# Score blocks of 64 queries by 192 keys, one bias product per PSUM bank, and the attention output copied out of PSUM by VectorE

## The chip, the cores and the metric

The kernel runs on one core of a Trainium2 chip. The metric is the device time of one execution in microseconds; the times shown are medians of a few runs. A core has five engines that run side by side and meet only at semaphores: TensorE (PE in the profile; its weight loads are PEld), VectorE (DVE), ScalarE (ACT), GpSimd (POOL) and SyncE (SP), which issues most of the transfers. Every engine works through its own instructions in the order in which they were written.

## The reference

For 8 batches and 8 heads there are 576 queries of width 64. A query sees itself and the 127 keys before it, with a penalty that grows with the distance and a slope for each head. The result goes through a soft mixture of experts with 8 experts of 4 slots.

```python
scores = scale * np.matmul(q, k.transpose(0, 1, 3, 2))
rel = pos[:, None] - pos[None, :]
bias = slopes[:, None, None] * (-np.abs(rel))[None, :, :]
mask = (rel >= 0) & (rel < window)                 # window = 128
scores = np.where(mask, scores + bias[None], -1000000000.0)
attn = softmax(scores)                             # rows
x = (attn @ v)                                     # all heads side by side: (4608, 512)

logits = x @ phi                                   # 32 slots
d = softmax(logits, axis=0); slot_input = d.T @ x
slot_out[e] = np.maximum(slot_input[e] @ w1[e], 0) @ w2[e]
return softmax(logits, axis=1) @ slot_out
```

## The kernel before, in words

A batch is cut into five tiles of queries: t = 0 to 3 with 128 queries, t = 4 with 64. A *group* is a tile and four of its heads (t < 4, g = 0 or 1), or tile 4 with all eight heads. There are nine groups a batch and 72 in all, and the main loop does one per iteration `i`, from about 9 to 210 us. The expert products and the output follow; they are not touched.

The scores of a group fill two PSUM banks, `s4s[i % 2]`, 128 partitions by 4 x 256 columns. Heads come in pairs: of a pair, one head lies on partitions 0 to 63 of the transposed queries and keys, the other on 64 to 127 (`par` in the code, which is also the bank), and `jj` counts the pairs of a group. For t > 0 the queries are cut into four strips of 32, and each strip meets 160 keys (`WIN = P + KB`), its own 32 and the 128 before. A strip has its own 32 of TensorE's columns, so its tile of the array is 64 rows by 32 columns, and eight tiles work side by side. Eight bias products with bf16 operands (`ones`, `ramp`; L259) start the sums, one for each strip and bank with 2 x 160 columns; then 16 f32 products of 160 columns follow (L266), each of which the trace shows as two. For t = 0 the 128 queries are one piece (L247, L252).

Since the strips are shifted against each other, each row's 128 valid keys lie in a ring of 256 columns. `merge` (L281 for t = 1 to 3, L283 for t = 4) folds the two halves into 128 columns by a predicated copy in PSUM. For t = 0 there are no older keys, and `merge` (L279) writes a very low number, `low`, over the keys that come after the query.

The rest of an iteration is a software pipeline in `softmax_front`, `expo`, `flip`, `split` and `values`:

- VectorE: `merge`, row maximum (`rowmax`, L301), reciprocal of the previous group's row sums (L313), the exponential's bias (L304), and the normalisation of the previous group's probabilities (L317).
- ScalarE: `split` of the group three back (L379, the flipped probabilities out of PSUM), the copies of the expert part (`x_keep`, L447, and others), `x_store` (L426), then four exponentials with row sums (L357).
- GpSimd: the row sums' total (L309), and two selects (L381, L383; for t = 4 L386, L388) that part the split probabilities into those of the tile's own keys and those of the tile before.
- TensorE: `flip` of the group three back (L372), `values` of the group four back (L410), the scores of the next group, then the expert part's products: `x_flip` (L438), `logits` (L456), `slot_sum` (L514).

`values` adds the two or four head pairs of a group into one PSUM bank `xp` for each tile. There is one such bank. When a tile's last group is done, `x_store` copies it to SBUF (37 times in the loop), and the next tile's `values` write the bank again. `x_store` is called by `after_values` behind `values`; without an engine in its call it uses VectorE. The loop body sets the order on every engine:

```python
if i:
    softmax_front(new, groups[i - 1])
...
flip(groups[i + near - FLAG]); split(groups[i + near - FLAG])
run("act", i)
values(groups[i + near - LAG]); after_values(i, groups[i + near - LAG])
scores(i + 1)
loads(i + 1)
expo(new)
run("pe", i); load_weights_at(i); run("dve", i)
```

`near` is 1 for the first seven iterations and 0 after; FLAG is 3 and LAG is 4. `run` issues what the expert part of a *pass* (four tiles together) has due in this iteration.

Of the kernel before, what the change touches and what calls it, by code (L numbers as in the profile page):

```python
# [10 lines left out]
F32 = mybir.dt.float32  # L11
# [13 lines left out]
P = 128  # L25
# [5 lines left out]
LOW = -1e30  # L31
# [3 lines left out]
KB = 32  # L35
# [33 lines left out]
def tile_attn_softmoe(  # L69
# [20 lines left out]
    mask_u = cst[:, 0:P].bitcast(I32)  # L90
    mask_t = cst[:, P:P + TAIL].bitcast(I32)
# [14 lines left out]
    ramp = cpool.tile([P, 2, 2, WIN], BF16, name="ramp")  # L106
    ones = cpool.tile([P, P], BF16, name="ones")
    area = cpool.tile([P, 19, HW], F32, name="area")

    kall = kq[:, 0:NB * P].rearrange("p (n j w) -> p n j w", n=NB, j=NPAIR)  # L110
    qs = [kq[:, NB * P + 2 * P * i:NB * P + 2 * P * i + 2 * P] for i in range(3)]
# [94 lines left out]
    with tc.manual_schedule(engines=ORDERED):  # L206
        warm = area[:, 2].bitcast(BF16)[:, 0:512]
        nc.vector.memset(warm, 0.0)
        nc.vector.memset(low, LOW)
        nc.vector.memset(ramp, 0.0)  # L210
        nc.vector.memset(ones, 1.0)
        nc.vector.memset(fine[:, 10:11], -1.0)
        nc.gpsimd.memset(cst[:, 0:P], 1.0)
        nc.gpsimd.affine_select(cst[:, 0:P], cst[:, 0:P], [[1, P]], ALU.is_gt, 0.0, base=0, channel_multiplier=-1)
        load_k(0, 0)
        load_q(0, nc.scalar)
        for par in range(2):
            nc.sync.dma_start(ramp[64 * par:64 * par + 1], slopes[par:par + 1])
# [12 lines left out]
        load_v()  # L231
        nc.scalar.dma_start(cst[:, P:], cstd)
        nc.scalar.dma_start(phi, phid)
        for t in range(2, NT):
            load_k(0, t)

    def scores(i):
        b, t, g = groups[i]
        s4 = s4s[i % 2]
        parts = [s4[:, 0:2], s4[:, 2:4]]  # L240
        if i == 0:
            parts = [ps_1.tile([P, 2, 2 * P], F32, tag="xp", name="s4_0"), pq[:, 0].rearrange("p (u w) -> p u w", u=2)]
            parts = parts[::-1]
        qt = qs[i % 3].rearrange("p (j w) -> p j w", w=width(t))
        if t == 0:
            for par, rows in enumerate(half):
                nc.tensor.matmul(  # L247
                    parts[par][:, :, 0:P], lhsT=ones[rows], rhs=ramp[rows, g, :, 0:P],
                    start=True, stop=False)
            for jj in range(2):  # L250
                for par, rows in enumerate(half):
                    nc.tensor.matmul(  # L252
                        parts[par][:, jj, 0:P], lhsT=qt[rows, jj], rhs=kall[rows, 0:4, 2 * g + jj],
                        start=False, stop=(jj == 1))
        else:
            strips = [(c // 2, c % 2) if t == 4 else (g, c) for c in range(4)]
            for par, rows in enumerate(half):
                for c, (h, r) in enumerate(strips):
                    nc.tensor.matmul(  # L259
                        s4[32 * c:32 * c + 32, 2 * par:2 * par + 2, 32 * r:32 * r + WIN],  # L260
                        lhsT=ones[rows, 0:32], rhs=ramp[rows, h], start=True, stop=False)
            for jj in range(2):
                for par, rows in enumerate(half):
                    for c, (h, r) in enumerate(strips):
                        m0 = 4 * (t - 1) + r
                        nc.tensor.matmul(  # L266
                            s4[32 * c:32 * c + 32, 2 * par + jj, 32 * r:32 * r + WIN],
                            lhsT=qt[rows, 2 * h + jj if t == 4 else jj, 32 * r:32 * r + 32],
                            rhs=kall[rows, m0:m0 + 5, 2 * h + jj], start=False, stop=(jj == 1))
        st[groups[i]] = {"s4": s4, "parts": parts}  # L270

    ALL, LO, HI = slice(0, 4), slice(0, 2), slice(2, 4)

    def merge(key, us=ALL):
        t = key[1]
        s4 = st[key]["s4"]
        if t == 0:
            m = len(range(4)[us])
            nc.vector.copy_predicated(merged(key, us), bc(mask_u, 1, m), bc(low, 1, m).to_broadcast([P, m, P]))  # L279
        elif t < 4:  # L280
            nc.vector.copy_predicated(s4[:, :, P:2 * P], bc(mask_u, 1, 4), s4[:, :, 0:P])  # L281
        else:
            nc.vector.copy_predicated(s4[:, :, 0:TAIL], bc(mask_t, 1, 4), s4[:, :, P:P + TAIL])  # L283
# [12 lines left out]
    def rowmax(key, us):
        if "mx" not in st[key]:
            o = P - merged_at(key)
            st[key]["mx"] = st[key]["s4"][:, :, o] if number[key] else work.tile([P, 4], F32, tag="mx", name="mx")
            st[key]["nb"] = work.tile([P, 4], F32, tag="nb", name="nb")  # L300
        nc.vector.tensor_reduce(st[key]["mx"][:, us], merged(key, us), axis=AX.X, op=ALU.max, negate=True)  # L301
# [49 lines left out]
    def expo(key, us=ALL):  # L351
        s = st[key]
        if "sm" not in s:
            s["p4"] = p4s[number[key] % 3]
            s["sm"] = work.tile([P, 4], F32, tag="sm", name="sm")
        for u in range(4)[us]:
            nc.scalar.activation(  # L357
                s["p4"][:, u], merged(key, u), AF.Exp,
                bias=s["nb"][:, u:u + 1], scale=SCALE, accum_out=s["sm"][:, u:u + 1],
            )  # L360

    def flip(key, us=ALL, to=None):
        s = st[key]
        if to is not None:
            s["pt"] = to.rearrange("p u (r w) -> p u r w", r=2)
            for u in range(4)[us]:
                nc.tensor.transpose(to[:, u], s["p4"][:, u], ident)
            return
        s["pt"] = pq_p.rearrange("p r (u w) -> p u r w", u=4)
        for u in range(4)[us]:  # L370
            for r, rows in enumerate(half):
                nc.tensor.transpose(s["pt"][:, u, r], s["p4"][rows, u], ident[rows, rows])  # L372

    def split(key, us=ALL):
        s, t = st[key], key[1]
        i = number[key] % 2 if number[key] < n - 1 else 2
        m = len(range(4)[us])
        pa, pp = pas[i], pps[i % 2]
        nc.scalar.copy(pa[:, us].rearrange("p u (r w) -> p u r w", r=2), s["pt"][:, us])  # L379
        if 0 < t < 4:  # L380
            nc.gpsimd.affine_select(  # L381
                pp[:, us], pa[:, us], [[0, m], [-1, P]], ALU.is_gt, 0.0, base=0, channel_multiplier=1)
            nc.gpsimd.affine_select(  # L383
                pa[:, us], pa[:, us], [[0, m], [1, P]], ALU.is_ge, 0.0, base=0, channel_multiplier=-1)
        elif t == 4:
            nc.gpsimd.affine_select(  # L386
                pp[:, us], pa[:, us], [[0, m], [0, 2], [-1, TAIL]], ALU.is_gt, 0.0, base=0, channel_multiplier=1)
            nc.gpsimd.affine_select(  # L388
                pa[:, us], pa[:, us], [[0, m], [0, 2], [1, TAIL]], ALU.is_ge, 0.0, base=0, channel_multiplier=-1)
        s.update(pd=pa, pp=pp)  # L390

    def values(key, pairs=None, to=None):
# [5 lines left out]
        pd, pp = st[key]["pd"], st[key]["pp"]  # L398
# [5 lines left out]
        for ph in parts:  # L404
            for i in inner:
                j = 2 * g + i
                for par in range(2):
# [4 lines left out]
                        rhs=src[:, 2 * par + i] if t < 4 else src[:, 2 * par + i % 2, TAIL * (i // 2):TAIL * (i // 2) + TAIL],  # L412
# [323 lines left out]
    def after_values(i, key):  # L736
# [8 lines left out]
        x_store(b, t, nc.scalar)  # L745
# [28 lines left out]
    with tc.manual_schedule(engines=ORDERED):  # L774
# [60 lines left out]
        split(gd, LO)  # L835
# [6 lines left out]
        split(gd, HI)  # L842
# [280 lines left out]
```

## Time and profile before

| | |
|---|---|
| median of 3 runs | 289.46 us (289.28 to 292.43) |
| the profiled execution | 288.49 us, its span 286.0 us |
| TensorE, VectorE, ScalarE, GpSimd busy | 253.9, 221.6, 205.6, 112.9 us |
| granted TensorE clock, mean | 0.982 |
| HBM | 251 GB/s over the span |

A row of the groups names line, engine, operation, output and input tile, with shapes as partitions x elements and the count. Behind the bar stand the busy time in us, the mean of one in ns, and the engine's idle time just ahead, with what ended it. For a product, 64*32 means 64 rows by 32 columns of weights. A row of the timeline has start, duration, engine and line, with the idle time in brackets; several instructions of one line are merged, with their count. A product's end is modelled, and the next one can begin before it. In a row of waits stand the total in us, the count and the longest. In the windows' row stand the length and the busy time of PE, PEld, DVE, ACT and POOL, then clock, DMA share and GB/s. "issue" is idle time for which the profile shows no reason.

### The profile page before, as it was taken

What the parts mean: (1) busy time and instruction counts of PE and PEld (TensorE: products, weight loads), DVE (VectorE), ACT (ScalarE), POOL (GpSimd) and SP (SyncE); (2) the same over time, 40 slices, a digit from 0 to 9 for tenths busy, and PEclk for the clock granted to TensorE, in tenths of its full rate; (3) what the DMA queues carried; (4) which work ended last, traced back from release to release, by engine and by line L of the source; (5) the groups of instructions that cost most, each with busy time, mean ns of one, the idle gap of its engine ahead of it and who ended that gap; (6) DMA issues with size and microseconds to landing.
All of it is one profiled execution on the core that took longest, in us unless ns stands there. A gap on an engine that the chain in (4) does not pass through costs nothing.

```text
span 286.0 us, 13588 instructions
## 1 busy us (share of the span) xinstructions
PE 253.9 (89%) x5535; PEld 178.9 (63%) x5535; DVE 221.6 (77%) x509; ACT 205.6 (72%) x817; POOL 112.9 (39%) x218
## 2 busy tenths in 40 slices
PE   8588999799979889989979998998979899999990
PEld 4366676676757567667657765766756443687750
DVE  2889989998997999988998998798973352656451
ACT  2888889988888988998898988888783411044460
POOL 2044626662573276257527725466552011000000
PEclk9689999999999999999999999999999999999997
DMA  6645368869885987969797978866574579998997
GB/s 184 218 134 164 100 197 270 276 195 289 285 271 152 305 297 233 278 224 305 218 286 242 328 236 251 278 204 219 165 265 140 169 254 365 411 393 322 362 384 282
DMA packets 36754, 72.61 MB, mean 254 GB/s; under 512 B 4402, under 2 KB 15316, under 8 KB 36692
## 3 DMA queue, kind: packets, MB, share of 16 engines
q1 hardware_dynamic: 35972, 71.24, 75.7%
q8 instruction: 43, 0.70, 1.0%
q10 hardware_dynamic: 720, 0.51, 0.6%
q14 instruction: 19, 0.16, 0.2%
HBM read 62.29 MB, written 9.44 MB: 251 GB/s over the span
## 4 chain that ended last, share of the span: by engine, by line
PE 45%; DVE 23%; ACT 16%; POOL 7%; issue 5%; DMA 2%; DVEq 0%; ACTq 0%; POOLq 0%
ACT area L357 9%; PE xp L410 7%; DVE area L317 6%; DVE s L301 6%; PE s L266 5%; PE op L967 5%; PE hp L930 5%; PE po L992 4%; DVE s L281 3%; POOL area L381 3%; PE pq L372 3%; PE lp L456 2%; DVE s L279 2%; PE s L259 2%; ACT area L379 2%
## 5 line engine op out<-in xcount | busy, mean ns | idle before, releaser
L357 ACT ACTIVATE area<-s,nb 128x128 f32<-128x128 f32 x286 | 102.7, 391 | 13.8 <-DVE nb L304 10.4
L410 PE MATMUL xp<-area 128*64 128x128 f32 (+1 forms) x1104 | 74.5, 272 | 8.4 <-POOL area L381 5.3
L357 ACT ACTIVATION_READ_ACCUMULATOR area<-s,nb 128x1 f32 x286 | 65.4, 229 | 0.0
L410 PEld LDWEIGHTS xp<-area 128*64 128x64 f32 x1104 | 54.1, 137 | 18.0 <-POOL area L381 6.1
L317 DVE TENSOR_TENSOR area<-area,rs 128x512 f32<-128x512 f32 (+1 forms) x73 | 61.0, 836 | 1.6
L301 DVE TENSOR_REDUCE s<-s 128x4 f32<-128x512 f32 x71 | 49.5, 697 | 2.2
L379 ACT COPY area<-pq 128x512 f32<-128x512 f32 (+1 forms) x72 | 43.5, 605 | 10.7 <-PE pq L372 9.0
L266 PE MATMUL s<-kq 64*32 64x160 f32 x1792 | 43.8, 302 | 2.3 <-issue 2.3
L309 POOL TENSOR_SCALAR rs<-sm 128x4 f32<-128x4 f32 x70 | 15.0, 214 | 73.0 <-ACT area L357 71.6
L383 POOL TENSOR_SCALAR_AFFINE_SELECT area<-area 128x512 f32<-128x512 f32 x48 | 41.7, 870 | 3.3
L381 POOL TENSOR_SCALAR_AFFINE_SELECT area<-area 128x512 f32<-128x512 f32 x48 | 35.5, 740 | 15.5 <-ACT area L379 14.6
L281 DVE COPY_PREDICATED s<-cst,s 128x512 f32<-128x512 int32 x48 | 33.1, 689 | 6.1 <-PE s L266 5.6
L372 PE MATMUL pq<-unit_r,area 64*128 64x64 f32 x552 | 31.3, 233 | 3.7 <-ACT area L322 2.8
L266 PEld LDWEIGHTS s<-kq 64*32 64x32 f32 x1792 | 30.1, 107 | 4.1 <-issue 3.5
L372 PEld LDWEIGHTS pq<-unit_r,area 64*128 64x128 f32 x552 | 23.3, 140 | 11.8 <-issue 3.2
L259 PE MATMUL s<-ramp,ones 64*32 64x320 bf16 x448 | 18.7, 311 | 4.8 <-ACT area L357 4.5
L426 ACT COPY area<-xp 128x512 f32<-128x512 f32 (+1 forms) x37 | 21.4, 578 | 0.2
L447 ACT COPY area<-pq 128x512 f32<-128x512 f32 x34 | 20.7, 608 | 0.3 <-PE pq L432 0.3
L438 PEld LDWEIGHTS pq<-unit_r,area 64*128 64x128 f32 x264 | 11.1, 137 | 12.8 <-issue 9.7
L994 ACT COPY ob<-po 128x512 f32<-128x512 f32 x19 | 10.4, 591 | 11.4 <-PE po L992 11.4
L994 DVE COPY ob<-po 128x512 f32<-128x512 f32 x17 | 11.2, 686 | 6.6 <-PE po L992 6.5
L438 PE MATMUL pq<-unit_r,area 64*128 64x64 f32 x264 | 15.2, 233 | 0.9 <-ACT area L379 0.6
(173 smaller groups left out, 329.1 us busy)
## 6 DMA issues: line engine op xcount, KB each, us to landing
w<-w SPq DMA_DIRECT2D x53, 512.0 KB, 5.5
out<-ob SPq DMA_DIRECT2D x36, 256.0 KB, 3.9
kq<-q_t SPq DMA_DIRECT2D x69, 128.0 KB, 3.5
kq<-k_t SPq DMA_DIRECT2D x32, 256.0 KB, 3.9
area<-v_n SPq DMA_DIRECT2D x31, 256.0 KB, 4.2
area<-w SPq DMA_DIRECT2D x8, 512.0 KB, 4.6
area<-v_n SPq DMA_DIRECT2D x12, 128.0 KB, 4.4
kq<-w SPq DMA_DIRECT2D x3, 512.0 KB, 5.9
```

What stands on the lines that cost most here:

```text
L259: nc.tensor.matmul(s4[32 * c:32 * c + 32, 2 * par:2 * par + 2, 32 * r:32 * r + WIN], lhsT=ones[rows, 0:32], rhs=ramp[rows, h], start=True, ...
L266: nc.tensor.matmul(s4[32 * c:32 * c + 32, 2 * par + jj, 32 * r:32 * r + WIN], lhsT=qt[rows, 2 * h + jj if t == 4 else jj, 32 * r:32 * r + 32],
L281: nc.vector.copy_predicated(s4[:, :, P:2 * P], bc(mask_u, 1, 4), s4[:, :, 0:P])
L301: nc.vector.tensor_reduce(st[key]["mx"][:, us], merged(key, us), axis=AX.X, op=ALU.max, negate=True)
L317: nc.vector.tensor_tensor(p4, p4, bc(rs, 2, P), op=ALU.mult)
L357: nc.scalar.activation(s["p4"][:, u], merged(key, u), AF.Exp, bias=s["nb"][:, u:u + 1], scale=SCALE, accum_out=s["sm"][:, u:u + 1],)
L372: nc.tensor.transpose(s["pt"][:, u, r], s["p4"][rows, u], ident[rows, rows])
L379: nc.scalar.copy(pa[:, us].rearrange("p u (r w) -> p u r w", r=2), s["pt"][:, us])
L381: nc.gpsimd.affine_select(pp[:, us], pa[:, us], [[0, m], [-1, P]], ALU.is_gt, 0.0, base=0, channel_multiplier=1)
L383: nc.gpsimd.affine_select(pa[:, us], pa[:, us], [[0, m], [1, P]], ALU.is_ge, 0.0, base=0, channel_multiplier=-1)
L410: nc.tensor.matmul(xp[D * par:D * par + D, j, 0:w], lhsT=v_slot[b, t - 1 + ph][:, D * h:D * h + D], rhs=src[:, 2 * par + i] if t < 4 else ...
L438: nc.tensor.transpose(xq[:, j, r], x[rows, j], ident[rows, rows])
```

## The change

`KB` goes from 32 to 64. A score block is now 64 queries by 192 keys. In a group of t < 4 a bank holds two pairs' heads on its two partition halves and the two query halves side by side: columns 0 to 191 for the first 64 queries, 192 to 383 for the second. For t = 4, where the 64 queries are one block, the second piece is another head pair, from column 256. The bias of a whole bank is one product: `pair_of` is a 128-wide bf16 weight that gives each partition half the slope of its head, and `ramp` is read with a window that slides by 64. For t = 0 a third row of the two adds the very low number to the columns of keys that don't exist, so that `merge` has the same form as elsewhere. Eight products of 64x64 weights and 192 columns follow; for t = 0 the first four have 64 columns and the others 128.

On TensorE, an iteration in which a tile's value products (`xp`) are followed by a group's scores (`s_0_83`, `s_1_84` are the two score buffers, `pq` the flips' bank) has before:

```order
L410 MATMUL xp<-area 64x128 x8
L259 LDWEIGHTS ones
L259 MATMUL s_1_84<-ramp,ones 32x2x160
...
L266 MATMUL s_1_84<-kq 32x160 x16
L372 MATMUL pq<-unit_r,area 128x64 x8
```

with eight pairs of the two L259 rows, and now:

```order
L407 MATMUL xp<-area 64x128 x8
L259 LDWEIGHTS pair_of
L259 MATMUL s_1_84<-ramp,pair_of 128x384
L259 LDWEIGHTS pair_of
L259 MATMUL s_1_84<-ramp,pair_of 128x384
L267 MATMUL s_1_84<-kq 64x192 x8
L371 MATMUL pq<-unit_r,area 128x64 x8
```

The order of the steps is the same; 24 products of a slot became ten.

A block's 192 keys need folding only in the 64 oldest and the 64 newest, so `merge` copies 2 x 2 x 64 elements of a row instead of 4 x 128 (and as many as before for t = 4).

`x_store` in `after_values` loses its engine, so that the copy (L421 now) is VectorE's. On VectorE in the second batch, around the first group of t = 1, before:

```order
L281 COPY_PREDICATED s_1_84<-cst,s_1_84 128x4x128
L301 TENSOR_REDUCE s_1_84<-s_1_84 128x4
L313 RECIPROCAL rs<-rs 128x4
L304 TENSOR_SCALAR nb<-s_1_84 128x4
L317 TENSOR_TENSOR area<-area,rs 128x512
L281 COPY_PREDICATED s_0_83<-cst,s_0_83 128x4x128
```

and now:

```order
L283 COPY_PREDICATED s_1_84<-cst,s_1_84 128x2x2x64
L297 TENSOR_REDUCE s_1_84<-s_1_84 128x2x2
L310 RECIPROCAL rs<-rs 128x4
L301 TENSOR_SCALAR nb<-s_1_84 128x4
L314 TENSOR_TENSOR area<-area,rs 128x512
L421 COPY area<-xp 128x512
L283 COPY_PREDICATED s_0_83<-cst,s_0_83 128x2x2x64
```

The copy of `xp` stands between a group's normalisation and the next merge, and waits for the tile's last value products. On ScalarE it stood ahead of the exponentials; in the same stretch, before:

```order
L379 COPY area<-pq 128x512
L447 COPY area<-pq 128x512
L426 COPY area<-xp 128x512
L357 ACTIVATE area,sm<-s_0_83,nb 128x128 x4
L379 COPY area<-pq 128x512
```

and now:

```order
L377 COPY area<-pq 128x512
L444 COPY area<-pq 128x512
L356 ACTIVATE area,sm<-s_0_83,nb 128x128 x4
L377 COPY area<-pq 128x512
```

The copy of `xp` is gone from ScalarE, and the exponentials follow the expert part's copy (L447, now L444) directly.

The probabilities of a group now have pairs on partition halves and query halves in the columns, so `flip` writes its results to other columns, `values` reads its moving operand in two pieces of 64, and the selects step over 64 instead of 128. At the start, two small loads for `ramp` and two for `pair_of` stand on SP's queue where two were, and the mask on GpSimd takes four selects instead of one.

```diff
-KB = 32
+KB = 64
+def slide(ap):
+    return bass.AP(ap.tensor, ap.offset, [list(ap.ap[0]), [KB, 2], [1, WIN]])
...
         for par in range(2):
-            nc.sync.dma_start(ramp[64 * par:64 * par + 1], slopes[par:par + 1])
+            nc.sync.dma_start(ramp[64 * par:64 * par + 3], slopes[par, :, 2 * P:])
+            nc.sync.dma_start(pair_of[64 * par:64 * par + 3], slopes[par, :, 0:2 * P])
...
     def scores(i):
...
-            for par, rows in enumerate(half):
-                for c, (h, r) in enumerate(strips):
-                    nc.tensor.matmul(
-                        s4[32 * c:32 * c + 32, 2 * par:2 * par + 2, 32 * r:32 * r + WIN],
-                        lhsT=ones[rows, 0:32], rhs=ramp[rows, h], start=True, stop=False)
-            for jj in range(2):
-                for par, rows in enumerate(half):
-                    for c, (h, r) in enumerate(strips):
-                        m0 = 4 * (t - 1) + r
-                        nc.tensor.matmul(
-                            s4[32 * c:32 * c + 32, 2 * par + jj, 32 * r:32 * r + WIN],
-                            lhsT=qt[rows, 2 * h + jj if t == 4 else jj, 32 * r:32 * r + 32],
-                            rhs=kall[rows, m0:m0 + 5, 2 * h + jj], start=False, stop=(jj == 1))
+        second = WIN if t < 4 else 2 * P
+        for par, rows in enumerate(half):
+            if t < 4:
+                dst, src = parts[par][:, 0:2 * WIN], slide(ramp[rows, g])
+            else:
+                dst, src = parts[par].rearrange("p (u w) -> p u w", u=2)[:, :, 0:WIN], ramp[rows, :, 0:WIN]
+            nc.tensor.matmul(dst, lhsT=pair_of[rows, int(t == 0)], rhs=src, start=True, stop=False)
+        for u in range(2):
+            h, hp = (u, g) if t < 4 else (0, u)
+            skip = max(2 * (1 - t) - h, 0)
+            m0 = 2 * (t - 1) + h
+            for par, rows in enumerate(half):
+                for jj in range(2):
+                    j = 2 * hp + jj
+                    nc.tensor.matmul(
+                        parts[par][KB * jj:KB * jj + KB, second * u + KB * skip:second * u + WIN],
+                        lhsT=qt[rows, jj if t < 4 else j, KB * h:KB * h + KB], rhs=kall[rows, m0 + skip:m0 + 3, j],
+                        start=False, stop=(u == 1))
...
     def merge(key, us=ALL):
...
-        if t == 0:
-            m = len(range(4)[us])
-            nc.vector.copy_predicated(merged(key, us), bc(mask_u, 1, m), bc(low, 1, m).to_broadcast([P, m, P]))
-        elif t < 4:
-            nc.vector.copy_predicated(s4[:, :, P:2 * P], bc(mask_u, 1, 4), s4[:, :, 0:P])
-        else:
-            nc.vector.copy_predicated(s4[:, :, 0:TAIL], bc(mask_t, 1, 4), s4[:, :, P:P + TAIL])
+        if key[1] < 4:
+            to, of, keep = x[:, :, 0:6:5], x[:, :, 2:4], bc(mask.bitcast(I32), 1, m)
+        else:
+            to, of, keep = x[:, :, 0:8:4], x[:, :, 2:8:4], bc(bc(mask[:, 0].bitcast(I32), 1, 2), 1, m)
+        nc.vector.copy_predicated(to, keep, of)
...
     def values(key, pairs=None, to=None):
...
-                        rhs=src[:, 2 * par + i] if t < 4 else src[:, 2 * par + i % 2, TAIL * (i // 2):TAIL * (i // 2) + TAIL],
+                        rhs=src[:, :, par, i] if t < 4 else src[:, i // 2, par, i % 2],
...
     def after_values(i, key):
...
-        x_store(b, t, nc.scalar)
+        x_store(b, t)
```

More of the change, by code (lines that the diff above doesn't have):

```diff
@@ L105, in tile_attn_softmoe @@
     kq = cpool.tile([P, 3 * UW], F32, name="kq")
[L106 to L107 removed]
+    ramp = cpool.tile([P, 2, 2 * P], BF16, name="ramp")
+    pair_of = cpool.tile([P, 2, P], BF16, name="pair_of")
     area = cpool.tile([P, 19, HW], F32, name="area")
[L110 to L111 removed]
+    kall = kq[:, 0:NPAIR * S].rearrange("p (n j w) -> p n j w", n=NB, j=NPAIR)
+    qs = [kq[:, NPAIR * S + 2 * P * i:NPAIR * S + 2 * P * i + 2 * P] for i in range(3)]
     half = [slice(64 * par, 64 * par + 64) for par in range(2)]
@@ L210, in tile_attn_softmoe @@
         nc.vector.memset(ramp, 0.0)
-        nc.vector.memset(ones, 1.0)
+        nc.vector.memset(pair_of, 0.0)
         nc.vector.memset(fine[:, 10:11], -1.0)
-        nc.gpsimd.memset(cst[:, 0:P], 1.0)
-        nc.gpsimd.affine_select(cst[:, 0:P], cst[:, 0:P], [[1, P]], ALU.is_gt, 0.0, base=0, channel_multiplier=-1)
+        nc.gpsimd.memset(mask, 1.0)
+        for c in range(2):
+            rows = slice(KB * c, KB * c + KB)
+            nc.gpsimd.affine_select(
+                mask[rows, 0], mask[rows, 0], [[-1, KB]], ALU.is_ge, 0.0, base=0, channel_multiplier=1)
+            nc.gpsimd.affine_select(
+                mask[rows, 1], mask[rows, 1], [[1, KB]], ALU.is_gt, 0.0, base=0, channel_multiplier=-1)
         load_k(0, 0)
@@ L296, in rowmax, with ranges @@
+    def ranges(key, us):
+        if number[key] == 0:
+            return st[key]["parts"][us.start // 2].unsqueeze(1)
+        return st[key]["s4"]
+    def merged(key, us):
+        return ranges(key, us).rearrange("p a (u w) -> p a u w", u=2)[:, :, :, 0:P]
     def rowmax(key, us):
-        if "mx" not in st[key]:
-            o = P - merged_at(key)
-            st[key]["mx"] = st[key]["s4"][:, :, o] if number[key] else work.tile([P, 4], F32, tag="mx", name="mx")
+        if "nb" not in st[key]:
@@ L306, in total @@
+        nc.vector.tensor_scalar_mul(nb, st[key]["mx"], SCALE)
     def total(key, us, eng=None):
@@ L1053, in constants @@
     slope = 2.0 ** (-8.0 * (np.arange(H, dtype=np.float64) + 1) / H)
-    slopes = (slope.reshape(2, 2, 2, 1).transpose(2, 0, 1, 3) / SCALE * np.arange(WIN)).astype(BF16_NP)
+    ramp = np.zeros((2, 3, 2, 2 * P))
+    ramp[:, 0:2] = slope.reshape(2, 2, 2, 1).transpose(2, 1, 0, 3) / SCALE * np.arange(2 * P)
+    ramp[:, 2, :, 0:P] = LOW
+    pair_of = np.zeros((2, 3, 2, P))
+    for jj in range(2):
+        pair_of[:, jj, :, KB * jj:KB * jj + KB] = 1.0
+    pair_of[:, 2, 1] = 1.0
+    slopes = np.concatenate([pair_of.reshape(2, 3, 2 * P), ramp.reshape(2, 3, 4 * P)], axis=2).astype(BF16_NP)
     r = np.arange(P)
     cst = np.zeros((P, TAIL + NS), np.float32)
-    cst[:, 0:TAIL] = np.arange(TAIL)[None, :] <= (r % TAIL)[:, None]
     cst[:, TAIL:] = np.arange(NS)[None, :] == (r % NS)[:, None]
```

76 lines of the change are left out of this document (29 added, 47 removed).

## The prediction, made before the changed kernel ran

> **What bounds the kernel now.** I first read the page's busy times, then the stretch from 9 to 210 us, in which the 72 score groups run, by windows.
>
> ```profile
> PE 253.9 (89%) x5535; PEld 178.9 (63%) x5535; DVE 221.6 (77%) x509; ACT 205.6 (72%) x817; POOL 112.9 (39%) x218
> 9.00:210.00 201.00, 183.33 (x4562) 134.79 (x4562) 183.49 (x405) 177.57 (x747) 104.57 (x192) 0.98 0.75 234
> ```
>
> The averages over the span mislead: in these 201 us TensorE is busy 183.3, VectorE 183.5 and ScalarE 177.6. Three engines are within 3% of each other. After 210 us the change touches nothing that counts. The chain of waits over the same window, and what VectorE and TensorE wait for in it:
>
> ```profile
> by line: ACT area L357 12.1%; PE xp L410 9.8%; DVE area L317 8.3%; PE s L266 7.7%; DVE s L301 7.7%; DVE s L281 4.5%; issue 4.5%; POOL area L381 3.8%; PE pq L372 3.8%; PE lp L456 3.5%; DVE s L279 3.3%; PE s L259 3.3%; ACT area L379 3.0%; POO
> DVE s L281 <- PE s L266: 5.6, 8, 1.4
> DVE rs L313 <- POOL rs L309: 4.0, 12, 0.6
> DVE nm L469 <- ACT lg L464: 3.3, 6, 0.8
> PE xp L410 <- POOL area L381: 5.3, 6, 1.4
> PE s L259 <- ACT area L357: 4.5, 9, 1.3
> ```
>
> The chain changes engine all the time, and no wait is long. So a change is worth what it takes off or puts on the chain, not its whole busy time.
>
> **TensorE: the score slot.** Here are TensorE's instructions in order of time, around two groups of t = 1 to 3 and one of t = 0, and then the groups by form (count, busy us, mean ns).
>
> ```profile
> 99.80 0.74 PE L266 MATMUL s<-kq 64*32 64x160 f32 x32
> 100.47 0.46 PE L438 MATMUL pq<-unit_r,area 64*128 64x64 f32 x8
> 100.77 0.41 PE L372 MATMUL pq<-unit_r,area 64*128 64x64 f32 x8
> 101.11 1.44 PE L410 MATMUL xp<-area 128*64 128x128 f32 x16
> 102.48 0.33 PE L259 MATMUL s<-ramp,ones 64*32 64x320 bf16 x8
> 102.63 0.73 PE L266 MATMUL s<-kq 64*32 64x160 f32 x32
> 105.70 0.28 PE L247 MATMUL s<-ramp,ones 64*128 64x256 bf16 x2
> 105.82 0.61 PE L252 MATMUL s<-kq 64*128 64x128 f32 x8
> ...
> L259 PE MATMUL s<-ramp,ones 64*32 64x320 bf16 x448 | 18.7, 311 | 4.8 <-ACT area L357 4.5
> L266 PE MATMUL s<-kq 64*32 64x160 f32 x1792 | 43.8, 302 | 2.3 <-issue 2.3
> L514 PE MATMUL ap<-area,dn 128*32 128x512 f32 x62 | 8.5, 605 | 0.0
> ```
>
> Of a mean, (605 - 302)/(512 - 160) = 0.86 ns goes with each column; the other 302 - 160 x 0.86 = 164 ns is a tail that overlaps the next product. One round of 160 columns is then 0.138 us, and the 32 products of a slot (16 products, each of f32 in two) are 4 rounds on eight array tiles: 4 x 0.138 + 0.165 = 0.72, measured 0.73. The slot lasts from 102.48 to 103.36, 0.88 us.
>
> After the change there are 16 products of 192 columns on four tiles, again 4 rounds, of 0.165: +0.11. The bias product has 384 columns for 320, at 0.43 ns (L259's 320 bf16 columns take as long as L266's 160 f32): +0.03. The third term is a change of form between bias (64x128 weights) and scores (64x64), which the old slot doesn't have, as both are 64x32. Its price: L438 starts 0.07 before the modelled end of L266 (100.54), L410 0.07 before that of L372 (101.18), but L372, of L438's form, 0.16 before L438's end (100.93). So a change of form costs 0.09 to 0.10. The first eight products behind it take 0.46 and not 0.41, for weights that couldn't be loaded ahead: 0.05, of which I take half as the new weights have half the columns. Sum 0.11 + 0.03 + 0.10 + 0.02 = **+0.26 us** a slot. The trace has no step from 64x128 to 64x64; the nearest rows bound the form term by 0 (L438 to L372) and 0.15, and I take 0.12 because each pair that differs in form shows it. [...]
>
> For t = 0 the slot was 0.73 (105.70 to 106.43) without a change of form. Now the bias has 128 columns more (+0.05), the form changes (+0.12), and the rounds go from four of 128 columns to two of 64 and two of 128 (-0.11): +0.06. In all TensorE gets 56 x 0.26 + 16 x 0.06 = 15.5 us more. On the chain L266's 7.7% and L259's 3.3% of 201 us are 22.1 us, some 26 slots at 0.84: **+6.8**.
>
> **VectorE: merge and copy.** These are the groups by form that change, with the nearest rows for what is new.
>
> ```profile
> L281 DVE COPY_PREDICATED s<-cst,s 128x512 f32<-128x512 int32 x48 | 33.1, 689 | 6.1 <-PE s L266 5.6
> L279 DVE COPY_PREDICATED s<-cst,fine 128x512 f32<-128x512 int32 x15 | 14.9, 997 | 0.1
> L283 DVE COPY_PREDICATED s<-cst,s 128x256 f32<-128x256 int32 x8 | 3.4, 422 | 0.3 <-PE s L266 0.3
> L424 DVE COPY area<-xp 128x512 f32<-128x512 f32 x1 | 0.7, 677 | 0.0
> L426 ACT COPY area<-xp 128x512 f32<-128x512 f32 x30 | 18.5, 616 | 0.1
> L426 ACT COPY area<-xp 128x256 f32<-128x256 f32 x7 | 2.9, 419 | 0.1
> L317 DVE TENSOR_TENSOR area<-area,rs 128x512 f32<-128x512 f32 x70 | 59.7, 853 | 1.4
> ```
>
> Every merge now has 256 elements, the form of L283: 48 x (689 - 422) = 12.8 and 15 x (997 - 422) = 8.6 us less. The 37 copies of x come to VectorE, 30 x 0.68 (L424's form) and 7 x 0.42: 23.3 more. So VectorE's work grows by 1.9, and ScalarE's falls by 18.5 + 2.9 = 21.4. Maximum, reciprocal and normalisation keep their sizes.
>
> On the chain, L281's 4.5% is 9.0 us, 14 merges at 0.65: **-3.7**. L279's 3.3% is 6.6 us, 7 merges: **-4.0**. For ScalarE's copies and VectorE's normalisations the chain has 9 and 18 pieces, the first and last of each:
>
> ```profile
> 44.38 0.47 ACT area L426
> 168.53 0.41 ACT area L426
> 18.08 0.69 DVE area L317
> 207.88 0.90 DVE area L317
> ```
>
> The nine copies (mean 0.44) go: **-3.9**. The new copy stands right behind the normalisation in 37 of 70 iterations, so behind 9 of the 18 on the chain: 9 x 0.68 = **+6.1**.
>
> Could the copy cost more than 0.68 here, where GpSimd runs beside it? From the timeline:
>
> ```profile
> 106.51 1.12 DVE L279 COPY_PREDICATED s<-cst,fine 128x512 f32<-128x512 int32 x1
> 106.11 0.97 POOL L383 TENSOR_SCALAR_AFFINE_SELECT area<-area 128x512 f32<-128x512 f32 x1
> 104.23 0.70 DVE L301 TENSOR_REDUCE s<-s 128x4 f32<-128x512 f32 x1
> 104.42 0.64 POOL L383 TENSOR_SCALAR_AFFINE_SELECT area<-area 128x512 f32<-128x512 f32 x1
> 102.99 0.87 DVE L317 TENSOR_TENSOR area<-area,rs 128x512 f32<-128x512 f32 x1
> 104.41 1.36 PE L410 MATMUL xp<-area 128*64 128x128 f32 x16 [0.66 <-POOL area L381]
> ```
>
> Beside a GpSimd select L279, with two inputs in SBUF, takes 1.12; L301, which reads PSUM, stays at 0.70. The copy reads PSUM alone, so I take 0.68; the other bound is 1.1, +3.8 on nine copies. [...]
>
> **The new wait.** Next tile's value products (L410, first half) write the bank that the copy reads. ScalarE copied as soon as the products ended; VectorE first finishes the normalisation, and behind the waiting copy stand the pass's sums and the next merge. In the rows above L317 ends at 103.86, 0.27 earlier with the shorter merge; a copy would end at 104.27, and L410 starts at 104.41, held by GpSimd. There the wait is hidden. Where GpSimd is in time it would not be, by 0.2 at most from this tile's distances: 0 to 37 x 0.2 = 7.4 us, of which I take a sixth, **+1.2**, since the one tile shown has none.
>
> **Edits with no price.** GpSimd's selects have the same 512 elements. The values' moving operand lies in two pieces of 64 columns; L266's lies in five pieces of 32 and fits the straight line above. Transposes and exponentials keep count and size. At the start SP issues two more small loads; its queue and the first q load are read here:
>
> ```profile
> 1.56 0.59 SPq L218 DMA_DIRECT2D ramp<-slopes  x2
> 4.54 0.28 PEld L252 LDWEIGHTS pq<-kq 64*128 64x128 f32 x1 [0.34 <-DMA kq<-q_t]
> ```
>
> An issue is 0.3, so the bias operands come some 0.6 later, of which the wait for q hides 0.34; the rest, 0.3, is paid back by the two half-size merges of group 0. The first k load behind them is also 0.6 later, and group 2, which needs it, has VectorE's whole first groups as cover. If that cover were gone it would cost 0.6 once.
>
> **Sum.** +6.8 - 3.7 - 4.0 - 3.9 + 6.1 = +1.3 on the old chain, +1.2 for the wait, so +2.5. The profiled execution took 288.5 us (span 286.0), the median of the runs is 1.0 above it: 289.5 + 2.5 = **292.0 us**.
>
> **Rivals.**
>
> *ScalarE's relief counts (faster).* VectorE waits 5.6 + 4.0 + 3.3 = 12.9 us in the window, half of it for ScalarE's exponentials and copies. If the copies fall into such gaps, the 6.1 and the 1.2 aren't paid: 2.5 - 7.3 = -4.8, 284.7. For it: 21.4 us less on ScalarE, in whose queue the copy stands ahead of the next exponentials. Against it: TensorE's load grows in the same stretch. It decides where VectorE still waits for GpSimd's row sums less than now but not more for scores.
>
> *TensorE becomes the bound (slower).* 183.3 + 15.5 = 198.8 busy, and its waits for GpSimd (5.3) and ScalarE (4.5) stay: 208.6 for 201, +7.6, 297.1. For it: TensorE hasn't 18 us of idle time in the window. Against it: part of its busy time is tail, and a later TensorE waits less.
>
> *The form change isn't charged inside a slot.* Then 26 x 0.12 = 3.1 go: 288.9.
>
> **How the numbers follow.** The forecast gets 0.48, the faster rival 0.20, TensorE 0.22, no form charge 0.10. A measurement of this kernel can tell about 1% from no change, here 286.6 and 292.4. Faster: 0.16 of the first rival and 0.04 of the others' edges, 0.20. Slower: nearly all of TensorE's 0.22, and 0.21 of the forecast, whose centre is close to the limit, 0.43. Within: 0.37. The range takes in both rivals, 284.5 to 298; the forecast's own, with the copy's and the wait's bounds, is 289 to 296.
>
> **What would show it.** Merges at 0.42 and copies at 0.68 on VectorE, ScalarE's busy time down by 21, score products near 330 ns with an idle step ahead of each slot's first. If I am right, VectorE's merge waits more often for scores, and first value products of a tile for the copy. If VectorE's waits shrink and its busy share rises, the first rival is right; if TensorE's idle time falls under 8 us, the second. Score products under 300 ns, or copies near 1.0, would make the sum wrong.

## The result and the profile after

The changed kernel takes 291.44 us in the median (289.40 to 292.62, 20 runs) and the kernel before 289.33 us (286.43 to 293.87, 20 runs). The ratio is 1.010, with a 95% interval of 1.0078 to 1.0123. So the change costs about 1%, and the forecast of 292.0 us was 0.6 us off. The kernel before spreads over 7 us, so each ratio here is made without the disturbed runs and can differ by up to 1% from the quotient of two medians.

The page's busy times and its chain of waits, of the profiled execution after (291.2 us, span 289.4):

```profile
PE 267.8 (93%) x4431; PEld 179.0 (62%) x4431; DVE 219.9 (76%) x546; ACT 191.5 (66%) x780; POOL 111.5 (39%) x221
PE 61%; DVE 22%; ACT 8%; issue 3%; DMA 2%; POOL 1%; DVEq 0%; ACTq 0%; SPq 0%; POOLq 0%
```

TensorE's busy time grew from 253.9 to 267.8 us, by 13.9; its idle time in the span fell from 286.0 - 253.9 = 32.1 to 21.6, by 10.5. The difference, 3.4, is what the span grew. So the new work went three quarters into TensorE's own gaps. The windows' row of the loop, the chain by line in it, and the waits that the prediction spoke of:

```profile
9.00:212.00 203.00, 194.71 (x3452) 134.27 (x3446) 181.52 (x441) 162.93 (x707) 102.14 (x192) 1.00 0.73 231
```

```profile
by line: PE xp L407 20.2%; PE s L267 14.9%; DVE area L314 9.5%; DVE s L297 6.0%; ACT area L356 5.7%; PE pq L371 5.5%; PE s L259 5.2%; DVE area L421 4.9%; PE pq L435 3.7%; PE lp L453 3.5%; DVE s L283 3.1%; issue 3.0%; PE ap L511 2.5%; DMA ar
```

```profile
PEld s L267 <- issue: 12.2, 69, 0.3
DVE s L283 <- PE s L267: 6.0, 13, 1.4
DVE area L421 <- PE xp L407: 4.2, 7, 0.8
PE xp L407 <- DVE area L421: 3.6, 8, 0.7
DVE rs L310 <- POOL rs L306: 2.2, 9, 0.9
```

TensorE is idle for 203.0 - 194.7 = 8.3 us of the loop; before it was 17.7 of 201. On the chain value products and scores (L407, L267, L259) hold 40.3%, where the lines that answer to them held 9.8 + 7.7 + 3.3 = 20.8%. The kernel whose chain changed engine all the time has become one that TensorE carries. The weights of L267 wait for "issue" 69 times, about once a slot: in the slot at 101.44 us below, their loads begin at 101.71, with the first product and 0.17 us behind the bias weights' loads. In the kernel before, L266's begin at 102.50, 0.13 ahead of the first product. I read the wait as the change of form; the kernel with one form, further down, doesn't have it. In the timeline of TensorE and in the groups by form:

```profile
101.44 0.34 PE L259 MATMUL s<-ramp,pair_of 64*128 64x384 bf16 x2
101.71 0.88 PE L267 MATMUL s<-kq 64*64 64x192 f32 x16
102.52 0.46 PE L435 MATMUL pq<-unit_r,area 64*128 64x64 f32 x8
105.94 1.21 PE L407 MATMUL xp<-area 128*64 128x128 f32 x16 [0.21 <-DVE area L421]
```

```profile
L267 PE MATMUL s<-kq 64*64 64x192 f32 x896 | 51.2, 345 | 0.0
L283 DVE COPY_PREDICATED s<-cst,s 128x256 f32<-128x256 int32 x71 | 29.9, 422 | 6.9 <-PE s L267 6.0
L421 DVE COPY area<-xp 128x512 f32<-128x512 f32 x31 | 21.2, 683 | 4.2 <-PE xp L407 4.2
L421 DVE COPY area<-xp 128x256 f32<-128x256 f32 x7 | 2.9, 417 | 0.0
```

A slot now runs from 101.44 to 102.59, 1.15 us for 0.88: +0.27, forecast +0.26. The scores start 0.27 behind the bias products' start. A bias product of 384 columns takes 0.165 at the prediction's 0.43 ns a column, an estimate (the mean of 343 ns here and the 289 ns of L247's 256 columns before give 0.42), so the step is 0.10, as forecast. Merges take 0.422 and copies 0.683, as forecast. Two sizes are off a little: a score product takes 345 ns for some 330 foretold, and a slot of t = 0 (107.08 to 107.92 in the same timeline) 0.84 us for 0.73, so +0.11 where +0.06 was forecast. The operations have about the predicted sizes; the open question is what each is worth.

### The profile page after: what moved, and what is told of

The parts are those of the page before. It is cut to its first block, busy times and chain, and to the rows that moved or that the text cites. A ratio compares the mean times of both kernels' runs of the same rounds, so it can differ in the third digit from the quotient of the medians.

```text
span 289.4 us, 11387 instructions
## 1 busy us (share of the span) xinstructions
PE 267.8 (93%) x4431; PEld 179.0 (62%) x4431; DVE 219.9 (76%) x546; ACT 191.5 (66%) x780; POOL 111.5 (39%) x221
## 4 chain that ended last, share of the span: by engine, by line
PE 61%; DVE 22%; ACT 8%; issue 3%; DMA 2%; POOL 1%; DVEq 0%; ACTq 0%; SPq 0%; POOLq 0%
PE xp L407 15%; PE s L267 10%; DVE area L314 7%; PE op L964 5%; ACT area L356 5%; PE hp L927 5%; DVE s L297 4%; PE pq L371 4%; PE s L259 4%; PE po L989 4%; DVE area L421 3%; PE pq L435 3%; PE lp L453 2%; DVE s L283 2%; PE ap L511 2%
## 5 line engine op out<-in xcount | busy, mean ns | idle before, releaser
L407 PE MATMUL xp<-area 128*64 128x128 f32 (+1 forms) x1104 | 71.4, 270 | 5.7 <-DVE area L421 3.6
L356 ACT ACTIVATION_READ_ACCUMULATOR area<-s,nb 128x1 f32 x286 | 62.2, 217 | 0.0
L407 PEld LDWEIGHTS xp<-area 128*64 128x64 f32 x1104 | 54.4, 137 | 12.2 <-POOL area L385 2.6
L267 PE MATMUL s<-kq 64*64 64x192 f32 (+2 forms) x1144 | 60.9, 328 | 0.0
L383 POOL TENSOR_SCALAR_AFFINE_SELECT area<-area 128x512 f32<-128x512 f32 (+1 forms) x57 | 43.8, 769 | 30.3 <-ACT area L377 29.7
L297 DVE TENSOR_REDUCE s<-s 128x4 f32<-128x512 f32 (+1 forms) x72 | 50.0, 694 | 2.2
L385 POOL TENSOR_SCALAR_AFFINE_SELECT area<-area 128x512 f32<-128x512 f32 (+1 forms) x57 | 45.2, 793 | 3.9
L267 PEld LDWEIGHTS s<-kq 64*64 64x64 f32 x1144 | 35.2, 137 | 14.3 <-issue 12.6
L283 DVE COPY_PREDICATED s<-cst,s 128x256 f32<-128x256 int32 (+1 forms) x72 | 30.2, 420 | 6.9 <-PE s L267 6.0
L371 PE MATMUL pq<-unit_r,area 64*128 64x64 f32 x552 | 31.5, 233 | 1.2 <-ACT area L319 0.8
L421 DVE COPY area<-xp 128x512 f32<-128x512 f32 (+1 forms) x38 | 24.1, 634 | 4.2 <-PE xp L407 4.2
L259 PE MATMUL s<-ramp,pair_of 64*128 64x384 bf16 x143 | 25.0, 343 | 1.4 <-ACT area L356 0.8
L444 ACT COPY area<-pq 128x512 f32<-128x512 f32 x34 | 20.1, 592 | 0.3 <-PE pq L429 0.3
L991 ACT COPY ob<-po 128x512 f32<-128x512 f32 x19 | 10.4, 591 | 11.4 <-PE po L989 11.4
L259 PEld LDWEIGHTS <-pair_of 64*128 64x128 bf16 x144 | 7.4, 93 | 15.2 <-issue 11.4
```

Source lines behind the costliest of these rows:

```text
L259: nc.tensor.matmul(dst, lhsT=pair_of[rows, int(t == 0)], rhs=src, start=True, stop=False)
L267: nc.tensor.matmul(parts[par][KB * jj:KB * jj + KB, second * u + KB * skip:second * u + WIN], lhsT=qt[rows, jj if t < 4 else j, KB * h:KB ...
L283: nc.vector.copy_predicated(to, keep, of)
L297: nc.vector.tensor_reduce(st[key]["mx"], merged(key, us), axis=AX.X, op=ALU.max, negate=True)
L356: nc.scalar.activation(s["p4"][:, u], src, AF.Exp, bias=s["nb"][:, u:u + 1], scale=SCALE, accum_out=s["sm"][:, u:u + 1],)
L371: nc.tensor.transpose(s["pt"][:, 2 * (u % 2) + u // 2, r], s["p4"][rows, u], ident[rows, rows])
```

## The experiments

**The two halves of the change, apart.** First the copy on VectorE, in the kernel before:

```diff
-        x_store(b, t, nc.scalar)
+        x_store(b, t)
```

> The old scores, with only the copy of x moved to VectorE. By the prediction's terms: 3.9 us of ScalarE's copies leave the chain, 6.1 of VectorE's copies and 1.2 of the new wait come onto it, so +3.4 us over the kernel before, about 292.7, ratio 1.012. If ScalarE's relief is what counts and the copies fall into VectorE's gaps: -3.9, about 285.4, ratio 0.987.

Measured: 298.57 us, ratio 1.0386 (1.0275 to 1.0497), some 11 us. Both theories were wrong: the first is some 8 us too low, the second has the wrong sign. The chain and a wait of the loop (9 to 210 us):

```profile
PE 43%; DVE 37%; ACT 9%; issue 5%; POOL 2%; DMA 1%; DVEq 0%; ACTq 0%; POOLq 0%
```

```profile
PE xp L410 <- DVE area L424: 12.4, 14, 1.7
```

VectorE's share of the chain rises from 23% to 37%, and TensorE waits 12.4 us for the copy to free `xp`, up to 1.7 us each time. Then the score blocks alone, in the changed kernel:

```diff
-        x_store(b, t)
+        x_store(b, t, nc.scalar)
```

> The new score blocks and merges, with the copy of x left on ScalarE. By the prediction's terms: +6.8 for the slots, -3.7 and -4.0 for the merges, so -0.9, about 288.4, ratio 0.997. If TensorE is the bound of the changed kernel, it gains nothing from the copy's place: as slow as the changed kernel, about 291.4, ratio 1.007. If ScalarE has to be relieved for the new blocks to pay, slower than the changed kernel, 293 or more.

Measured: 290.66 us, 1.0077 (1.0035 to 1.0119). This fits the second theory, TensorE as the bound. The page's busy times and chain:

```profile
PE 269.5 (93%) x4431; PEld 178.9 (62%) x4431; DVE 203.5 (70%) x509; ACT 205.7 (71%) x817; POOL 113.2 (39%) x221
PE 71%; ACT 9%; DVE 8%; POOL 6%; issue 3%; DMA 1%; DVEq 0%; ACTq 0%; SPq 0%; POOLq 0%
```

VectorE has 18.1 us less to do than before (203.5 for 221.6), and TensorE 15.6 more (269.5 for 253.9), and the kernel is slower. The halves cost 3.9% and 0.8% alone and 1.0% together, so they don't add: behind the new blocks the same copy costs 0.2%, which these intervals can't tell from nothing.

**Is VectorE's time free there?** The kernel above (copy on ScalarE), with a second predicated copy of half a merge behind each merge, which writes the same values again:

```diff
         nc.vector.copy_predicated(to, keep, of)
+        if number[key]:
+            nc.vector.copy_predicated(to[:, 0], keep[:, 0], of[:, 0])
```

> New score blocks with the copy of x on ScalarE, and half of each merge done a second time, which changes nothing in the result: 71 x 0.29 = 20.6 us more on VectorE, as much as the shorter merges had saved (21.4). By the prediction's terms the saving was worth 7.7: 7.4 us slower than the same kernel without it, about 298, ratio 1.033. If TensorE bounds the new blocks, VectorE's time is free there: at most 2 us slower, 292.5, ratio 1.014.

Measured: 292.29 us, 1.0053 (1.0027 to 1.0078). The added group, and the page's chain:

```profile
L285 DVE COPY_PREDICATED s<-cst,s 128x128 f32<-128x128 int32 x71 | 21.0, 296 | 2.4
```

```profile
PE 57%; DVE 26%; ACT 6%; POOL 5%; issue 2%; DMA 1%; DVEq 0%; ACTq 0%; SPq 0%; POOLq 0%
```

21 us more on VectorE cost 1.6 us by the medians and nothing by the ratios, where the prediction's terms said 7.4. VectorE's time is nearly free there, whatever the chain's 26% say. With it the changed blocks keep VectorE busy for 221.0 us, as the kernel before does (221.6).

**A longer slot in the old blocks.** For t > 0, products of the form of L247 whose results the bias then overwrites; they put a change of form into each slot:

```diff
             for par, rows in enumerate(half):
+                nc.tensor.matmul(
+                    s4[:, 2 * par:2 * par + 2, 0:P], lhsT=ones[rows], rhs=ramp[rows, 0, :, 0:P], start=True, stop=True)
+            for par, rows in enumerate(half):
```

> The kernel before, with one more bias product per bank and group of t > 0, of 64x128 weights and 256 columns, ahead of the strips' own, which write over it: per slot 0.11 us of columns and one more change of form, 0.10, so 56 x 0.21 = 11.8 us on TensorE and nothing on VectorE. It prices the longer slot by itself. By the chain of the kernel before (26 slots on it): +5.5, ratio 1.019. If TensorE's idle time takes it: at most +1.5, ratio 1.005. If every slot counts: +11.8, ratio 1.041.

Measured: 298.16 us, 1.0269 (1.0198 to 1.0339). The timeline of TensorE at one slot, and the page's busy times (span 295.1):

```profile
103.67 0.28 PE L258 MATMUL s<-ramp,ones 64*128 64x256 bf16 x2
103.88 0.33 PE L262 MATMUL s<-ramp,ones 64*32 64x320 bf16 x8
104.03 0.73 PE L269 MATMUL s<-kq 64*32 64x160 f32 x32
PE 266.4 (90%) x5647; PEld 184.9 (63%) x5647; DVE 223.0 (76%) x509; ACT 206.5 (70%) x817; POOL 111.6 (38%) x218
```

The bias starts 0.21 later: 56 x 0.21 = 11.8 us of work cost about 7.8 us. With 26 slots on the chain they would have cost 26 x 0.21 = 5.5. TensorE's idle time fell only from 32.1 to 295.1 - 266.4 = 28.7, so its gaps took up far less than in the changed kernel, where it fell to 21.6. The new blocks add more work and cost only 2 us. VectorE's shorter merges don't explain that, since the kernel with the doubled merges is at 1.0053. Why the old blocks pay so much more stays open.

**The form change taken out.** In the changed kernel, each bias product as two with weights of 64x64, the form of the scores:

```diff
-            nc.tensor.matmul(dst, lhsT=pair_of[rows, int(t == 0)], rhs=src, start=True, stop=False)
+            for jj in range(2):
+                cols = slice(KB * jj, KB * jj + KB)
+                nc.tensor.matmul(
+                    dst[cols], lhsT=pair_of[rows, int(t == 0), cols], rhs=src, start=True, stop=False)
```

> The changed kernel, but a bank's bias is two products with 64x64 weights and 384 columns, on the partition halves, instead of one with 64x128: bias and scores have one form. If a change of form costs 0.12 us a slot inside the slot, the idle step ahead of the score products goes, and with about half of the 72 slots on the changed kernel's chain it takes off 3.6 to 4.3 us: about 287.5, ratio 0.994. If the form change is not charged there, or only moves to the next step: unchanged, 291.4, ratio 1.007.

Measured: 286.67 us, 0.9953 (0.9916 to 0.9990): 1.5% less than the changed kernel, the first theory. The timeline of TensorE, a group by form, the page's chain, and a wait of the loop:

```profile
102.85 0.36 PE L261 MATMUL s<-ramp,pair_of 64*64 64x384 bf16 x4
103.04 0.82 PE L270 MATMUL s<-kq 64*64 64x192 f32 x16
```

```profile
L270 PE MATMUL s<-kq 64*64 64x192 f32 x896 | 47.5, 330 | 0.4 <-DMA kq<-k_t 0.4
```

```profile
PE 43%; DVE 37%; ACT 9%; DMA 4%; issue 3%; POOL 1%; DVEq 0%; ACTq 0%; POOLq 0%
```

```profile
PE xp L410 <- DVE area L424: 6.6, 11, 1.0
```

The scores start 0.19 behind the bias instead of 0.27, though there are twice as many bias products, and take 0.82 instead of 0.88: a slot of 1.01 us for 1.15. The scores' weights no longer wait for "issue". With TensorE relieved, the chain is shared with VectorE again, and its wait for the copy grows from 3.6 to 6.6 us. So the copy's engine should matter again. The same kernel with the copy on ScalarE:

```diff
-        x_store(b, t)
+        x_store(b, t, nc.scalar)
```

> As before this one, bias in the scores' form, and the copy of x on ScalarE. By the prediction's terms the two add: 291.4 - 3.6 - 3.4 = 284.4, ratio 0.983. If TensorE is the bound whatever the copy does: no more than the form change alone, 287.5, ratio 0.994.

Measured: 283.99 us, 0.9866 (0.9791 to 0.9940). That is nearer to the first theory: the copy's place is worth some 0.9% here, and all four runs (283.1 to 284.4) lie below the lowest with the copy on VectorE (285.5). And with the copy on ScalarE for odd t, on VectorE for even t:

```diff
-        x_store(b, t)
+        x_store(b, t, nc.scalar if t % 2 else None)
```

> Bias in the scores' form, and the copy of x shared: tiles t = 1 and 3 on ScalarE, t = 0, 2 and 4 on VectorE. If each copy has its price on its engine whatever the others do: between the two kernels of one form, about 285.3, ratio 0.991. If ScalarE (24% of the chain with all copies) and VectorE (37% with all copies) are each bound only with the whole load: below both, about 282.5, ratio 0.980.

Measured: 284.47 us, 0.9774 (0.9736 to 0.9812). The time lies between the two theories and the ratio below both, so neither is shown. The two kernels can't be told apart, and both beat the kernels before and after. The page's chain of the second:

```profile
PE 57%; DVE 17%; ACT 13%; issue 4%; POOL 3%; DMA 3%; DVEq 0%; ACTq 0%; SPq 0%; POOLq 0%
```

**The order of copy and normalisation.** The copy waits behind the normalisation on VectorE. Here the normalisation leaves `softmax_front` and follows `after_values`, in the kernel before with the copy on VectorE:

```diff
-        normalise(old, HI if first else ALL)
...
+            if i:
+                normalise(groups[i - 1], HI if i == 1 else ALL)
             if i + 1 < n:
```

> Old scores, the copy of x on VectorE, but ahead of the normalisation instead of behind it, so that the bank of the value products is free 0.85 us earlier. If the first experiment's cost is TensorE's wait for the copy (12.4 us in its profile): most of it goes, ratio 1.015 or less. If it is VectorE's 23.3 us of work on an engine without room: unchanged, ratio 1.035 or more.

Measured: 294.81 us, 1.0219 (1.0139 to 1.0299), between the two. TensorE's wait for the copy in the loop, which was 12.4 us with the copy behind the normalisation:

```profile
PE xp L409 <- DVE area L423: 1.3, 3, 0.6
```

Nearly the whole wait is gone, but of the 3.9% only some 1.7 points: these are the order. The other 2.2 come from something else that the copy does on VectorE in the old blocks; the runs don't separate it. The same edit in the changed kernel:

> The changed kernel with the copy of x ahead of the normalisation. It takes away the wait of a tile's first value products for the copy (3.6 us of TensorE's idle time in the changed kernel's profile), which the prediction priced at 1.2. By that price: 290.2, ratio 1.006. If the whole wait is on a chain that is TensorE's for 61%: 2.2 off, 289.2, ratio 1.003. If normalising later costs as much as copying earlier gains: unchanged, ratio 1.010.

Measured: 291.55 us, 1.0084 (1.0043 to 1.0125), not to be told from unchanged (1.010). The page's chain, and the copy's wait in the loop:

```profile
PE 74%; DVE 9%; ACT 5%; POOL 4%; issue 3%; DMA 2%; DVEq 0%; SPq 0%; ACTq 0%; POOLq 0%
```

```profile
DVE area L420 <- PE xp L406: 11.4, 19, 1.4
```

TensorE's wait for the copy is gone from its list, and the copy waits for TensorE instead, 11.4 us for 4.2. A wait of 3.6 us was removed and bought nothing that shows. That the later normalisation costs what the earlier copy gains, the third theory, isn't ruled out. In the kernel with mixed copies the order gives nothing either:

> Bias in the scores' form, copies of t = 1 and 3 on ScalarE and the others on VectorE, there ahead of the normalisation. In the profile without the last step TensorE waits 4.2 us for the copy and is 57% of the chain: 2 us less than 284.5, about 282.3, ratio 0.973. If the wait only moves to the normalisation: unchanged, 284.5, ratio 0.979.

Measured: 284.50 us, 0.9819 (0.9746 to 0.9892), unchanged.

**The granted clock.** On record, the clock of the kernel before is 0.53 from 9 to 12.5 us and 0.50 from there to 16; the changed kernel's is 1.00, though its products are slow there too (last section). To keep TensorE busy through it, 37 products that nobody reads were put into iterations 1 to 7 of the kernel before:

```diff
+IDLE = {1: 10, 2: 8, 3: 5, 4: 4, 5: 4, 6: 3, 7: 3}
...
+            for _ in range(IDLE.get(i, 0)):
+                nc.tensor.matmul(idle, lhsT=ones[half[0]], rhs=ramp[half[0], 0, :, 0:P], start=True, stop=True)
```

> The kernel before with 37 products in iterations 1 to 7 whose results nobody reads, at the end of TensorE's part of an iteration, so that it isn't idle there. In the profile of before TensorE's clock is granted at 0.50 to 0.53 from 9 to 16 us, and 37 runs of that kernel lose 1.8 us for each 0.01 of mean clock. If idle time at the start is what lowers the clock and the clock is what the old kernel loses: clock 0.99 and 2.5 us less, ratio 0.991. If the clock doesn't depend on it, or VectorE sets that stretch's pace: unchanged or, by the 4.9 us of products, up to 2 us slower, ratio 1.00 to 1.007.

Measured: 291.96 us, 1.0097 (1.0050 to 1.0144). The windows of its start:

```profile
12.50:16.00 3.50, 3.50 (x40) 2.45 (x24) 2.28 (x6) 1.51 (x8) 0.19 (x1) 0.50 0.39 114
16.00:20.00 4.00, 4.00 (x103) 2.66 (x101) 2.24 (x5) 2.31 (x10) 0.73 (x2) 0.75 0.12 37
```

The stretch at half clock was still there (0.50 from 12.5 to 16 us), so the run doesn't answer what it was made for; it only shows that the products cost something themselves. As many products of that form in the mixed kernel with the copy ahead:

> The one before it with 37 products in iterations 1 to 7 whose results nobody reads. Its clock would otherwise be near 0.988. If the clock at the start still costs: 0.5 to 1 us less, 281.5, ratio 0.970. If not: unchanged, 282.3, ratio 0.973.

Measured: 285.75 us, 0.9837 (0.9790 to 0.9884), no better than without them. Here the clock on record from 9 to 210 us is 1.00, which need not hold for the start; the last section returns to it.

## Why the prediction was right

The time was right, but only part of the reasons, so it was in good part luck. By its own steps:

- **The sizes** (slot +0.26, form 0.10 + 0.02, merges 0.42, copies 0.68, a wait of TensorE for the copy) held: 1.15 - 0.88 = 0.27, 0.10, 0.422, 0.683, and 3.6 us of waits where a bound of 0 to 7.4 was given. What makes the step of 0.10 from 64x128 to 64x64 isn't shown, but with bias and scores in one form the scores start 0.19 behind the bias, and all but 0.02 of that are its columns (0.165). "The form change isn't charged inside a slot" is out. Taking it away gave 1.5%, some 4.3 us, more than the 3.1 us priced for it: without it the change is no loss (0.9953).
- **The merges, -3.7 and -4.0,** failed. Score blocks alone were to give +6.8 - 7.7 = -0.9 us; they cost 0.8%, some 2.2. The step that failed is that merges on the old chain are still on it afterwards. 21 us put back on VectorE cost 0 to 1.6 us, not 7.4.
- **The copy, +6.1 + 1.2 - 3.9 = +3.4,** failed in both directions. In the old blocks it costs 11 us: TensorE waits 12.4 us for `xp`, not 1.2, and some 5 us of the cost go with that wait; the other 6 are not explained. In the new ones it costs 0.7 by the ratios (1.0100 for 1.0077), not clear of nothing, although it has 4.9% of the loop's chain, 9.9 us.
- **The slots, +6.8,** came out with a smaller price: TensorE's busy time grew by 13.9 and its gaps gave back 10.5. Only slots and merges together were measured, +2.2; with the shorter merges worth 0 to 1.6, the slots cost 2 to 4 us.
- So the sum +2.5 met the measured +2.1 (+2.9 by the ratio) because errors of both signs cancelled: a gain from the merges that was put 6 to 8 us too high, against charges for slots and copy that were too high by 3 to 5 and 2.7.
- **The rivals.** "ScalarE's relief counts" is out: the kernel isn't faster, and putting the copy back on ScalarE gains where anything moves. One of its signs was met: VectorE waits less for the row sums (2.2 for 4.0) and no longer for scores (6.0 for 5.6 + 0.3, the second for t = 4), though more often (13 times for 8 + 1). The other wasn't: VectorE's busy share fell from 77% to 76%. "TensorE becomes the bound" named the mechanism that the chain shows, and its mark, idle time under 8 us, was nearly met with 8.3. Its price, +7.6, was too high since it kept TensorE's waits for GpSimd (5.3) and ScalarE (4.5), and these went down as its "against" said.
- **ScalarE's busy time** was to fall by 21.4 and fell by 14.1 (205.6 to 191.5); **VectorE's** was to grow by 1.9 and fell by 1.7. Both forecasts took the sum of the copies' durations for busy time. But records of neighbouring instructions overlap: in the trace before, only 13.0 of the 21.4 us of copies are time in which no other ScalarE instruction is recorded, and in the trace after, 19.1 of the 24.1 us on VectorE.

## What to carry to other kernels

Shares of the old chain priced none of the larger edits here: -7.7 us for merges worth 0 to 1.6, +3.4 for a copy that cost 11 in the old blocks, +5.5 for a longer slot that cost 7.8. When the new blocks added some 15 us to TensorE's work for 18 us of gaps, the chain moved there, and what other engines saved or paid was then nearly free. So sum the work of each engine against its gaps first, and ask which engine is left as the bound. That sum gives no price by itself: the longer old slot added 11.8 us to the same gaps and cost far more than the new blocks. Look then at the most frequent step on that engine: here two weights of 64 columns instead of one of 128 took out a change of form, more instructions took less time (a slot of 1.01 us for 1.15), and with the copy back on ScalarE, wholly or half, the change became a gain of 1.3 to 2.3%.

## What the runs showed of the hardware

I had not expected stretches at half clock in a kernel whose TensorE is busy 89% of the span. The rows of the clock over the span's 40 slices, of the kernel before and of the one after, and windows at the start of each:

```profile
PEclk9689999999999999999999999999999999999997
```

```profile
12.50:16.00 3.50, 3.50 (x87) 2.23 (x66) 2.78 (x6) 2.54 (x13) 0.19 (x1) 0.50 0.39 104
```

```profile
PEclk9999999999999999999999999999999999999995
```

```profile
12.50:16.00 3.50, 3.50 (x36) 2.12 (x34) 2.48 (x6) 2.40 (x13) 0.19 (x1) 1.00 0.24 57
```

In the kernel before, a stretch of 6.83 us near the start (9.24 to 16.07) is granted half the clock. A slot's scores in it, in the timeline of TensorE, take 1.31 us instead of 0.73:

```profile
12.02 1.31 PE L266 MATMUL s<-kq 64*32 64x160 f32 x32
```

The 1.00 of the kernel after in the window above isn't what its products show. Its clock is on record only from 17.20 us on; a slot's scores at 12.55 us take 1.56 us and those at 18.69 us 0.88, and a score product of 192 columns takes 533 ns in the mean from 9 to 17 us and 335 from 18 to 212. So its start is slow as well, and the mean clock leaves that out. The kernel before is on record from 5.83 us and starts slow too: its first product of L247, at 4.09, takes 0.37 us for a mean of 0.289.

In these two traces the clock on record is 1.00 or 0.50 and nothing else. Before, it changes at 9.24, 16.07 and 282.31 us, 6.83 and 266.24 us apart, and after, 266.24 us lie between 17.20 and 283.44: 2 and 78 times 3.41. The kernel before with the copy on VectorE has a mean clock of 0.97 from 9 to 210 us, for 0.98 without that.

The traces also show what comes ahead of such a stretch. Here are two windows of 3.41 us and the one behind each, first of the kernel before with the copy on VectorE, then of the one with the longer slot:

```profile
58.62:62.03 3.41, 1.72 (x40) 1.20 (x44) 3.26 (x7) 2.21 (x10) 3.19 (x5) 1.00 0.85 260
62.03:65.44 3.41, 3.41 (x68) 2.71 (x54) 2.77 (x6) 2.36 (x11) 1.71 (x4) 0.50 0.47 169
```

```profile
206.35:209.76 3.41, 1.76 (x56) 1.15 (x52) 0.74 (x2) 2.46 (x11) 1.47 (x3) 1.00 0.31 99
209.76:213.17 3.41, 3.41 (x92) 2.43 (x76) 3.03 (x7) 2.45 (x10) 1.73 (x3) 1.00 0.37 92
```

Behind 1.72 us of recorded busy time (51%) the clock is halved, behind 1.76 (52%) it isn't. In the kernel before, TensorE is busy for 1.40 us (41%) of the window ahead of the stretch, 5.83 to 9.24. Of the windows from 16.07 us to its last product the least busy, 80.92 to 84.33, has 1.90 us (56%), and the clock stays at 1.00. In the changed kernel the least busy one from 17.20 us on, ahead of the one with its last product, is 228.82 to 232.24 with 2.04 us (60%), and the clock stays at 1.00; but behind the window with the last product, 280.02 to 283.44, busy for 2.00 us (58%), it is halved. So no share of recorded busy time that parts the two cases is shown.

With 37 more products the stretch of the kernel before is about as long: clocks of 0.81 from 9 to 12.5 us, 0.50 to 16 and 0.75 to 20 make 6.8 us at half clock, by an estimate. And with the copy ahead, the changed kernel's clock on record from 9 to 212 us is 0.99 instead of 1.00.

What the clock is worth stays open. Over 34 runs of the kernel before, time and mean clock correlate at -0.52, with 1.0 us for each 0.01 of clock; the medians are 0.98 before and 0.99 after, both of the clock on record, which in the profiled executions leaves out a slow start. In the mixed kernel with the added products, two executions at 0.99 took 282.4 and 282.5 us, those at 0.98 took 285.1 to 285.9. But over the 20 runs of the changed kernel there is no correlation (0.03), and of the ten runs with the new blocks alone the five at 0.98 took 289.2 to 290.5 us and the five at 0.99 took 290.8 to 291.7. So whether the clock has a part in the measured +1% isn't shown, and no term of the prediction has it.
